# Two decode layers on one core: first keys as whole heads, w_down in four parts, last feed-forward in column halves, output turned on VectorE

## The chip, the cores and the metric

The kernel runs on one core of a Trainium2 chip. The metric is the device time of one execution in microseconds, lower is better; five executions of the kernel were timed. The profile shows one execution of its own: its span runs from the first to the last instruction, and its time is a little longer than its span.

## The reference, cut to what matters

Batch 4, one new token each, width D = 512, 32 query heads and 8 key/value heads of 128, 4096 cached positions, feed-forward width F = 1792. The same attention and feed-forward (same weights, same caches) are applied twice in a row. Softmax has scale 128 ** -0.5, gelu is the tanh approximation, and the layer norm has no gain or offset.

```python
def reference(A_x, A_k_cache, A_v_cache, A_wq, A_wo, B_x, B_w_gate, B_w_up, B_w_down):
    def _A_ref(x, k_cache, v_cache, wq, wo):
        q = (x @ wq).reshape(B, Sq, Hq, Dh).transpose(0, 2, 1, 3)
        k = jnp.repeat(k_cache, rep, axis=1)
        v = jnp.repeat(v_cache, rep, axis=1)
        scores = jnp.einsum("bhqd,bhkd->bhqk", q, k) * (Dh ** -0.5)
        o = jnp.einsum("bhqk,bhkd->bhqd", _softmax(scores), v)
        return o.transpose(0, 2, 1, 3).reshape(B, Sq, Hq * Dh) @ wo
    def _B_ref(x, w_gate, w_up, w_down):
        return (_gelu(x @ w_gate) * (x @ w_up)) @ w_down
    x = A_x
    for _ in range(2):
        x = x + _A_ref(_layernorm(x), A_k_cache, A_v_cache, A_wq, A_wo)
        x = x + _B_ref(_layernorm(x), B_w_gate, B_w_up, B_w_down)
    return x
```

## The kernel before

**Stages.** Each batch element has its own keys and values, some 8.4 MB of each, and they are too many to keep. So the kernel interleaves the two layers. `attend(None, 0)` (L498) does the first layer's attention of element 0. Then the loop at L679 does, for each element b, `dense(b, 1, ...)` (L660: rest of the output projection, layer norm, feed-forward), the query of the second layer, and `attend(b, b + 1, ...)`: the second layer's scores of element b against keys that still lie in SBUF, and the first layer's attention of element b + 1. `attend_last` (L618) ends the second layer's attention of element 3, and `dense(0, B, ...)` (L705) does the second feed-forward for all four elements at once. Values are read twice, once for each layer, and keys once.

**Order of work.** Nothing is scheduled by a tool: `tc.manual_schedule()` (L81) leaves the order of each engine as the program writes it. All loads go out on SP's queue (`dq`, L83) in program order, and a load waits there until its buffer is free. Work of one element's second layer is mixed by hand into the other's first layer: `fill(n)` in `dense` does n V tiles of the second layer, `vals.step(n)` n V tiles of the first.

**Keys.** A key head is two tiles of 128 partitions x 16 positions x 128 (512 KB, 4 KB a partition), `KT[head][t]` (L90). `Keys.load` (L361 on, issue at L365) issues them and `Keys.turn` (L367) transposes a tile in place in 32-bit blocks on VectorE (L372). Both run through `Keys.tile` (L356): per group of four heads, first t = 0 of the four, then t = 1. `scores(sc, g, t)` (L377) multiplies the four heads of a group for one t. For element 0, `attend` issues wq of group 0, the eight key tiles of group 0, wq of group 1, the eight of group 1, and then V tiles (L540 to L544).

**Values.** V tiles have seven buffers; `load_v` (L454) issues loads for as long as there is a free one, and `Values.step` (L467) frees one after its 16 matmuls (L481). In `attend_last` the key buffers serve for V tiles too (L625).

**Weights.** `load_rest` (L124) loads wo in four parts, w_gate and w_up whole, and w_down in three parts of 7, 4 and 3 row blocks of 128 rows. It is called in element 0's attention, after its last V tile is issued (L601).

**Feed-forward.** `ffn_in` (L300) has two forms. For one element, the activation is the stationary operand and the results are rows spread over the partitions, which `turn_rows` (L214) transposes on VectorE (L215). For four elements, the weights are the stationary operand and the result comes in columns (L307). `gelu` (L321) takes the columns through VectorE and ScalarE's tanh (L330), `gate_up` (L335) multiplies in the up half, and `down` (L343) runs 14 x 4 matmuls (L347). The layer norm's factor is made by `ln_rstd` (L183) in ten small VectorE instructions (L185 to L200), called in `dense` as an argument of `gelu`, which transposes the gate rows on entry:

```python
        sq, h = gelu(nb, rg, ln_rstd(nb, mv))
        H_bf = gate_up(nb, sq, h, ru)
```

**End.** The state `XX` holds the activations with the width on partitions. At the end `xoT` copies it to bf16 (L708), four transposes on TensorE put the batch on partitions (L711), VectorE copies them out of PSUM (L713), and SP stores 4 rows of 1 KB (L714).

## Time and profile before

| What | us |
| --- | --- |
| median of five runs | 316.14 |
| lowest and highest of them | 313.99, 318.96 |
| profiled execution, its own time | 318.96 |
| its span | 317.2 |
| TensorE matmuls busy | 213.7 (67%) |
| VectorE busy | 171.2 (54%) |
| ScalarE busy | 28.9 (9%) |
| 118 V tiles, median from issue to landing | 8.8 |
| 64 key tiles, median from issue to landing | 10.2 |

In the profile's lines, PE is a matmul and PEld its weight load, DVE is VectorE, ACT ScalarE, and SPq the issue of a DMA on SP's queue. A line of the timeline gives start and duration in us, engine, source line, operation, what it writes and reads with their shapes, a count, and in brackets how long the engine was idle before it and what ended that. A line of groups gives count, then busy us in total and mean ns of one. PEclk is the clock that TensorE was granted as a share of full, and the mean over the span was 0.692. Parts of a line's name can stand for several buffers, since buffer numbers are left out. An engine's busy share is a mean over stages with different limits, so stages are read one by one.

### The profile page before, as it was taken

How to read it: one execution, taken by the hardware profiler on the slowest of the kernel's cores; microseconds unless marked ns; L12 is line 12 of the kernel's file. 1: busy time of each engine (PE TensorE's matmuls, PEld its weight loads, DVE VectorE, ACT ScalarE, POOL GpSimd, SP SyncE). 2: the span in 40 equal slices, each digit the busy share in tenths (PEclk: the TensorE clock that was granted, in tenths of full speed). 3: DMA queues.
4: the chain of work that ended last, by engine and by line, in shares of the span. 5: the costliest groups of instructions: out<-in, count | busy, mean ns of one | idle time of the engine just before them, and what ended most of it. 6: DMA issues, size and time to landing. Idle time of an engine off the chain costs nothing.

```text
span 317.2 us, 8714 instructions
## 1 busy us (share of the span) xinstructions
PE 213.7 (67%) x3844; PEld 122.5 (39%) x3844; DVE 171.2 (54%) x481; ACT 28.9 (9%) x70; POOL 0.7 (0%) x6
## 2 busy tenths in 40 slices
PE   1460585343576669889946389699563797998875
PEld 0010344121324135656431246464421365645654
DVE  5575751023438896355378943354598552545133
ACT  0002010000002021200100212000202040003100
POOL 0000000000000000000000000000000000000000
PEclk9999999999998555555675555555855555559555
DMA  6999999999949999999999999999999999999910
GB/s 251 397 411 396 406 411 401 351 379 383 389 133 387 400 410 403 352 396 397 321 402 408 409 406 349 374 355 333 413 408 409 410 398 341 399 393 365 395 44 3
DMA packets 35527, 114.09 MB, mean 360 GB/s; under 512 B 3225, under 2 KB 9121, under 8 KB 35489
## 3 DMA queue, kind: packets, MB, share of 16 engines
q1 hardware_dynamic: 35488, 113.53, 94.2%
q8 instruction: 30, 0.49, 0.6%
q14 instruction: 9, 0.07, 0.0%
HBM read 113.51 MB, written 0.00 MB: 358 GB/s over the span
## 4 chain that ended last, share of the span: by engine, by line
DMA 46%; PE 25%; DVE 15%; SPq 8%; issue 3%; ACT 2%; DVEq 0%; ACTq 0%
DMA kt<-in_A_k_cache_dram 22%; DMA v<-in_A_v_cache_dram 21%; PE sc L383 6%; PE ot L481 6%; DVE kt L372 5%; DMA wd_sb<-in_B_w_down_dram 3%; SPq L127 3%; SPq L133 3%; PE rows L280 3%; PE rows L314 3%; PE y L347 2%; PE rows L225 2%; PE x L429 1%; DVE pp L410 1%; DVE rows L215 1%
## 5 line engine op out<-in xcount | busy, mean ns | idle before, releaser
L481 PEld LDWEIGHTS <-v 128*128 128x128 bf16 x1920 | 59.8, 105 | 51.2 <-DMA v<-in_A_v_cache_dram 26.1
L372 DVE STREAM_TRANSPOSE kt<-kt 128x1024 f32<-128x1024 f32 x64 | 74.9, 1216 | 7.2 <-DMA kt<-in_A_k_cache_dram 7.1
L481 PE MATMUL ot<-pe,v 128*128 128x4 bf16 x1920 | 63.7, 167 | 18.8 <-DMA v<-in_A_v_cache_dram 17.8
L383 PE MATMUL sc<-kt,qb 128*32 128x512 bf16 x512 | 63.9, 553 | 15.4 <-DVE kt L372 11.6
L215 DVE STREAM_TRANSPOSE rows<-rows 128x512 f32<-128x512 f32 (+1 forms) x23 | 16.3, 708 | 39.7 <-PE rows L225 19.9
L383 PEld LDWEIGHTS <-qb 128*32 128x32 bf16 x512 | 17.4, 117 | 46.3 <-issue 33.9
L402 ACT ACTIVATE pp<-sc,nm 128x512 bf16<-128x512 f32 x16 | 11.0, 688 | 155.6 <-DVE junk L398 155.5
L489 DVE TENSOR_TENSOR OT_bf<-ot,rden 128x8 bf16<-128x8 f32 (+1 forms) x40 | 6.5, 163 | 34.2 <-PE ot L481 33.7
L429 PE MATMUL x<-pp,ident_bf 128*32 128x128 bf16 x256 | 9.1, 282 | 23.3 <-DVE pp L410 23.2
L280 PE MATMUL rows<-wo_sb,OT_bf 128*1 128x512 bf16 (+1 forms) x136 | 17.2, 611 | 7.3 <-DMA wo_sb<-in_A_wo_dram 6.3
L225 PE MATMUL rows<-wq_sb,xn_bf 128*1 128x512 bf16 (+1 forms) x160 | 18.9, 622 | 4.8 <-DMA wq_sb<-in_A_wq_dram 4.5
L429 PEld LDWEIGHTS <-ident_bf 128*32 128x32 bf16 x256 | 6.7, 121 | 29.4 <-issue 27.8
L389 DVE TENSOR_REDUCE m<-sc 128x1 f32<-128x512 f32 x16 | 10.8, 676 | 12.1 <-PE sc L383 12.1
L410 DVE STREAM_TRANSPOSE pp<-pp 128x512 bf16<-128x512 bf16 x16 | 11.2, 702 | 4.7 <-ACT pp L402 4.3
L432 ACT CAST pe<-x 128x512 bf16<-128x512 f32 x16 | 9.4, 585 | 20.0 <-PE x L429 20.0
L246 PE MATMUL qe<-qm,t_bf 128*128 128x64 bf16 x16 | 3.5, 218 | 11.4 <-DVE qm L236 6.3
L347 PE MATMUL y<-H_bf,wd_sb 128*128 128x1 bf16 (+1 forms) x280 | 8.5, 166 | 2.7 <-DVE H_bf L340 1.5
L249 DVE TENSOR_TENSOR qb<-qe,amask 128x256 bf16<-128x256 f32 x16 | 6.8, 425 | 5.9 <-PE qe L246 5.9
L347 PEld LDWEIGHTS <-wd_sb 128*128 128x128 bf16 x280 | 8.1, 104 | 4.0 <-DMA wd_sb<-in_B_w_down_dram 3.0
L225 PEld LDWEIGHTS <-xn_bf 128*1 128x1 bf16 (+1 forms) x160 | 4.4, 110 | 13.1 <-issue 12.0
L415 PE MATMUL den<-zx,mean_f 128*128 128x16 f32 x32 | 8.9, 357 | 0.0
L420 DVE RECIPROCAL rden<-den 128x16 f32<-128x16 f32 x16 | 4.0, 251 | 8.5 <-PE den L415 8.0
(78 smaller groups left out, 125.0 us busy)
## 6 DMA issues: line engine op xcount, KB each, us to landing
v<-in_A_v_cache_dram SPq DMA_DIRECT2D x118, 512.0 KB, 8.8
kt<-in_A_k_cache_dram SPq DMA_DIRECT2D x64, 512.0 KB, 10.2
wq_sb<-in_A_wq_dram SPq DMA_DIRECT2D x2, 2048.0 KB, 7.8
wo_sb<-in_A_wo_dram SPq DMA_DIRECT2D x4, 1024.0 KB, 11.8
kt<-in_A_v_cache_dram SPq DMA_DIRECT2D x8, 512.0 KB, 10.4
wg_sb<-in_B_w_gate_dram SPq DMA_DIRECT2D x1, 1792.0 KB, 13.5
wu_sb<-in_B_w_up_dram SPq DMA_DIRECT2D x1, 1792.0 KB
wd_sb<-in_B_w_down_dram SPq DMA_DIRECT2D x1, 896.0 KB, 16.0
```

The lines of the kernel that those rows point to most:

```text
L127: dq.dma_start(out=wo_sb[:, i * n:(i + 1) * n], in_=wo_dram[:, i * n:(i + 1) * n])
L215: nc.vector.transpose(out=rows[:, :n], in_=rows[:, :n])
L225: nc.tensor.matmul(rows[j * QS:j * QS + nb, :], lhsT=xn_bf[:, k, bs], rhs=w, start=(k == 0), stop=(k == KD - 1))
L280: nc.tensor.matmul(rows[r0:r0 + lhsT.shape[-1], :], lhsT=lhsT, rhs=wo_sb[:, i, :], start=(start and n < QD), stop=(stop and n >= hp - QD))
L347: nc.tensor.matmul(y[:, k], lhsT=wd_sb[:, c, k * P:(k + 1) * P], rhs=H_bf[:, c, :], start=(c == 0 and k == 0), stop=(c == KF - 1), skip_gr ...
L372: nc.vector.transpose(out=words, in_=words)
L383: nc.tensor.matmul(sc[s * QS:(s + 1) * QS], lhsT=qb[:, w0:w0 + 2 * W], rhs=kt[:, :, be // 2, :, be % 2], start=(t == 0 and be == 0), stop= ...
L389: nc.vector.tensor_reduce(out=m[:], in_=sc.rearrange("p c j -> p (c j)"), axis=AX.X, op=ALU.max)
L402: nc.scalar.activation(out=pp[:], in_=sc[:], func=ACT.Exp, bias=nm[:, 0:1], scale=scale, accum_out=ls[:])
L410: nc.vector.transpose(out=flat, in_=flat)
L429: nc.tensor.matmul(x[a * QS:(a + 1) * QS, s], lhsT=ident_bf[:, s * QS:(s + 1) * QS], rhs=pT[:, a], start=True, stop=True, skip_group_check ...
L481: nc.tensor.matmul(self.ot[:, s % 2], lhsT=v[:, i, :], rhs=pe[:, s, c, :], start=(c == 0), stop=(c == C - 1), skip_group_check=True)
```

## The change

1. **Element 0's keys as whole heads.** The two tiles of a head become halves of one buffer `KH[head]`. Element 0's heads are loaded by `load_whole`, one load of 1 MB (8 KB a partition) each. `Keys.tile` runs head by head for element 0, and `attend` spreads the turns anew: seven before the first scores, one before the second, and so on. For later elements the loads are those of before.
2. **w_down in four parts** of 7, 3, 3 and 1 row blocks.
3. **Feed-forward functions.** `ffn_in` keeps only its row form. `gelu` now takes the turned gate columns as an argument ahead of the layer norm's factor, and writes into tiles that are made outside.
4. **The last feed-forward** is written out: gate in two halves of 7 column blocks, then gelu in two halves, then for each half the up matmuls and `gate_up`. `down` is as before.
5. **The last V tile** is loaded in two parts of 8 positions each.
6. **The output** is added straight into a bf16 tile `xo` with 16 used columns, turned by four 32 x 32 transposes on VectorE, and stored as 16 rows of 256 bytes.

```diff
@@ -87,7 +87,8 @@
     wg_sb = wts.tile([P, KD, F], BF16, name="wg_sb")
     wu_sb = wts.tile([P, KD, F], BF16, name="wu_sb")
     wd_sb = wts.tile([P, KF, D], BF16, name="wd_sb")
-    KT = [[wts.tile([P, CH, Dh], BF16, name=f"kt{i}_{t}") for t in range(NT)] for i in range(Hkv)]
+    KH = [wts.tile([P, C, Dh], BF16, name=f"kt{i}") for i in range(Hkv)]
+    KT = [[KH[i][:, t * CH:(t + 1) * CH] for t in range(NT)] for i in range(Hkv)]
     wq_dram = A_wq.rearrange("(k p) n -> p k n", p=P)
     wo_dram = A_wo.rearrange("(i p) n -> p i n", p=P)
 
@@ -97,6 +98,8 @@
     OT2_bf = state.tile([P, Hq, B], BF16, name="OT2_bf")
     q1_bf = state.tile([P, NG, NK, B], BF16, name="q1_bf")
     xn_bf = state.tile([P, KD, B], BF16, name="xn_bf")
+    xo = state.tile([P, QS], BF16, name="xo")
+    xr = state.tile([QS, P], BF16, name="xr")
     qb = state.tile([P, W + NK * 2 * W], BF16, name="qb")
 
     ROWS = [ps_row.tile([P, 512], FP32, name=f"rows{i}") for i in range(2)]
@@ -114,8 +117,11 @@
     def groups(b):
         return [b % NG, (b + 1) % NG]
 
+    def cache_rows(cache, b, kvh, c0, n):
+        return cache[b, kvh].rearrange("(p c) d -> p c d", p=P)[:, c0:c0 + n]
+
     def cache_tile(cache, b, kvh, t):
-        return cache[b, kvh].rearrange("(p c) d -> p c d", p=P)[:, t * CH:(t + 1) * CH]
+        return cache_rows(cache, b, kvh, t * CH, CH)
 
     def load_wq(g):
         n = HG * Dh
@@ -128,7 +134,7 @@
         dq.dma_start(out=wg_sb[:], in_=B_w_gate.rearrange("(k p) n -> p k n", p=P))
         dq.dma_start(out=wu_sb[:], in_=B_w_up.rearrange("(k p) n -> p k n", p=P))
         wd_dram = B_w_down.rearrange("(k p) n -> p k n", p=P)
-        cuts = [0, KF // 2, KF - 3, KF]
+        cuts = [0, KF // 2, KF - 4, KF - 1, KF]
         for lo, hi in zip(cuts, cuts[1:]):
             dq.dma_start(out=wd_sb[:, lo:hi], in_=wd_dram[:, lo:hi])
 
@@ -138,6 +144,7 @@
         for r in ROWS:
             nc.vector.memset(r[:], 0.0)
         nc.vector.memset(qb[:], 0.0)
+        nc.vector.memset(xo[:], 0.0)
         nc.vector.tensor_reduce(out=amask[:], in_=ident_bf[:].rearrange("p (a i) -> p a i", a=QD),
                                 axis=AX.X, op=ALU.max)
         nc.vector.tensor_reduce(out=s32_f[:], in_=ident_bf[:].rearrange("p (a i) -> p i a", a=QD),
@@ -297,48 +304,39 @@
             nc.vector.tensor_tensor(out=XX[:, 0, bs], in0=XX[:, 0, bs],
                                     in1=y.rearrange("p k b -> p b k"), op=ALU.add)
 
-    def ffn_in(b0, nb, w_sb, cols):
+    def ffn_in(b0, nb, w_sb):
         bs = slice(b0, b0 + nb)
         rows = new_rows()
-        if cols:
-            h = rows[:, :KF * nb].rearrange("p (c j) -> p c j", j=nb)
-            for c in range(KF):
-                for k in range(KD):
-                    nc.tensor.matmul(h[:, c], lhsT=w_sb[:, k, c * P:(c + 1) * P],
-                                     rhs=xn_bf[:, k, bs], start=(c == 0 and k == 0),
-                                     stop=(k == KD - 1), skip_group_check=True)
-            return h, cols
         for k in range(KD):
             w = w_sb[:, k].rearrange("p (n a i) -> p a n i", a=QD, i=QS)
             for j in range(QD):
                 nc.tensor.matmul(rows[j * QS:j * QS + nb, :KF * QS], lhsT=xn_bf[:, k, bs],
                                  rhs=w[:, j], start=(k == 0), stop=(k == KD - 1))
-        return rows, cols
-
-    def ffn_cols(h, nb):
-        return h[0] if h[1] else turn_rows(h[0], KF * QS)[:, :, :nb]
-
-    def gelu(nb, rows, rstd):
-        hg = ffn_cols(rows, nb)
-        h = small.tile([P, KF, nb], FP32, name="h", tag="h")
-        nc.vector.tensor_tensor(out=h[:], in0=hg, in1=spread_rstd(rstd, KF, nb), op=ALU.mult)
-        sq = small.tile([P, KF, nb], FP32, name="sq", tag="sq")
+        return rows
+
+    def ffn_cols(rows, nb):
+        return turn_rows(rows, KF * QS)[:, :, :nb]
+
+    def gelu(nb, hg, rstd, sq, h):
+        n = h.shape[1]
+        nc.vector.tensor_tensor(out=h[:], in0=hg, in1=spread_rstd(rstd, n, nb), op=ALU.mult)
         nc.vector.scalar_tensor_tensor(out=sq[:], in0=h[:], scalar=0.044715, in1=h[:],
                                        op0=ALU.mult, op1=ALU.mult)
         nc.vector.scalar_tensor_tensor(out=sq[:], in0=sq[:], scalar=1.0, in1=h[:],
                                        op0=ALU.add, op1=ALU.mult)
         nc.scalar.activation(out=sq[:], in_=sq[:], func=ACT.Tanh, scale=GELU_C)
         nc.vector.scalar_tensor_tensor(out=h[:], in0=h[:], scalar=0.5,
-                                       in1=spread_rstd(rstd, KF, nb), op0=ALU.mult, op1=ALU.mult)
-        return sq, h
-
-    def gate_up(nb, sq, h, rows):
-        hu = ffn_cols(rows, nb)
+                                       in1=spread_rstd(rstd, n, nb), op0=ALU.mult, op1=ALU.mult)
+
+    def ffn_tiles(nb):
+        sq = small.tile([P, KF, nb], FP32, name="sq", tag="sq")
+        h = small.tile([P, KF, nb], FP32, name="h", tag="h")
+        return sq, h, small.tile([P, KF, nb], BF16, name="H_bf", tag="H_bf")
+
+    def gate_up(hu, sq, h, H_bf):
         nc.vector.scalar_tensor_tensor(out=sq[:], in0=sq[:], scalar=1.0, in1=h[:],
                                        op0=ALU.add, op1=ALU.mult)
-        H_bf = small.tile([P, KF, nb], BF16, name="H_bf", tag="H_bf")
         nc.vector.tensor_tensor(out=H_bf[:], in0=hu, in1=sq[:], op=ALU.mult)
-        return H_bf
 
     def down(nb, H_bf):
         y = ps_sm.tile([P, KD, nb], FP32, name="y", tag="sm")
@@ -355,14 +353,20 @@
 
         def tile(self, n):
             o, u = divmod(n, TG)
-            t, s = divmod(u, GH)
+            s, t = divmod(u, NT) if self.b == 0 else divmod(u, GH)[::-1]
             return groups(self.b)[o] * GH + s, t
+
+        def load_whole(self, count):
+            for _ in range(count):
+                kvh = self.tile(self.nl)[0]
+                self.nl += NT
+                dq.dma_start(out=KH[kvh][:], in_=cache_rows(A_k_cache, self.b, kvh, 0, C))
 
         def load(self, count):
             for _ in range(count):
                 kvh, t = self.tile(self.nl)
                 self.nl += 1
-                dq.dma_start(out=KT[kvh][t][:], in_=cache_tile(A_k_cache, self.b, kvh, t))
+                dq.dma_start(out=KT[kvh][t], in_=cache_tile(A_k_cache, self.b, kvh, t))
 
         def turn(self, count=1):
             for _ in range(count):
@@ -458,7 +462,10 @@
                 return
             seen["load"] += 1
             v = held[b, g, s, t] = free.pop(0)
-            dq.dma_start(out=v[:], in_=cache_tile(A_v_cache, b, g * GH + s, t))
+            n = CH // 2 if seen["load"] == len(loads) else CH
+            for c in range(0, CH, n):
+                dq.dma_start(out=v[:, c:c + n],
+                             in_=cache_rows(A_v_cache, b, g * GH + s, t * CH + c, n))
 
     class Values:
         def __init__(self, b, last, prob, dst):
@@ -538,9 +545,9 @@
                 load_v()
         else:
             load_wq(0)
-            keys.load(TG)
+            keys.load_whole(GH)
             load_wq(1)
-            keys.load(TG)
+            keys.load_whole(GH)
             load_v()
             make_identity(nc, ident_bf[:])
             build_consts()
@@ -552,14 +559,15 @@
             rstd1 = ln_rstd(B, ln_center(0, B))
             q_first(q_rows(0, B, 0), 0, rstd1)
             build_q1(0, 0)
-            turn(4)
+            turn(TG - 1)
         sc1 = new_scores(0)
         scores(sc1, ga, 0)
-        turn(4)
+        turn(1 if first else GH)
         if two:
             vals2.step(max(early[b2] - vals2.n - 1, 0))
         scores(sc1, ga, 1)
-        turn()
+        if two:
+            turn()
         p0 = soft(sc1)
         turn()
         if two:
@@ -569,13 +577,15 @@
         turn()
         prob1[ga] = (pe, soft_recip(den))
         if first:
+            turn()
             q_first(q_rows(0, B, 1), 1, rstd1)
         build_q1(b1, gb)
-        turn()
+        turn(5 if first else 1)
         vals.step(2)
         sc1 = new_scores(0)
         scores(sc1, gb, 0)
-        turn(4)
+        if two:
+            turn(4)
         vals.step(3)
         scores(sc1, gb, 1)
         rows = new_rows()
@@ -665,11 +675,12 @@
         ln_square(b0, nb)
         mv = ln_center(b0, nb)
         fill(1)
-        rg = ffn_in(b0, nb, wg_sb, nb > 1)
+        rg = ffn_in(b0, nb, wg_sb)
         fill(1)
-        ru = ffn_in(b0, nb, wu_sb, nb > 1)
-        sq, h = gelu(nb, rg, ln_rstd(nb, mv))
-        H_bf = gate_up(nb, sq, h, ru)
+        ru = ffn_in(b0, nb, wu_sb)
+        sq, h, H_bf = ffn_tiles(nb)
+        gelu(nb, ffn_cols(rg, nb), ln_rstd(nb, mv), sq, h)
+        gate_up(ffn_cols(ru, nb), sq, h, H_bf)
         fill(2)
         add_y(b0, nb, down(nb, H_bf))
 
@@ -702,16 +713,35 @@
         else:
             proj = attend_last(b, next_q, fill)
 
-    dense(0, B, proj, lambda n: None)
-
-    xoT = state.tile([P, KD, B], BF16, name="xoT")
-    nc.vector.tensor_copy(out=xoT[:], in_=XX[:, 0].rearrange("p b k -> p k b"))
-    xo_ps = ps_sm.tile([P, D], BF16, name="xo_ps", tag="sm")
-    for k in range(KD):
-        nc.tensor.transpose(xo_ps[:B, k * P:(k + 1) * P], xoT[:, k, :], ident_bf[:, :])
-    xo = tmpp.tile([P, D], BF16, name="xo", tag="pp")
-    nc.vector.tensor_copy(out=xo[:B, :], in_=xo_ps[:B, :])
-    nc.sync.dma_start(out=out.flatten_outer_dims(), in_=xo[:B, :])
+    def ffn_part(w_sb, h, c0, c1):
+        for c in range(c0, c1):
+            for k in range(KD):
+                nc.tensor.matmul(h[:, c], lhsT=w_sb[:, k, c * P:(c + 1) * P], rhs=xn_bf[:, k, :],
+                                 start=(c == 0 and k == 0), stop=(k == KD - 1),
+                                 skip_group_check=True)
+
+    out_proj_end(*proj)
+    add_y(0, B, proj[0])
+    ln_square(0, B)
+    mv = ln_center(0, B)
+    hg, hu = [new_rows()[:, :KF * B].rearrange("p (c j) -> p c j", j=B) for _ in range(2)]
+    parts = [(0, KF // 2), (KF // 2, KF)]
+    for c0, c1 in parts:
+        ffn_part(wg_sb, hg, c0, c1)
+    rstd = ln_rstd(B, mv)
+    sq, h, H_bf = ffn_tiles(B)
+    for c0, c1 in parts:
+        gelu(B, hg[:, c0:c1], rstd, sq[:, c0:c1], h[:, c0:c1])
+    for c0, c1 in parts:
+        ffn_part(wu_sb, hu, c0, c1)
+        gate_up(hu[:, c0:c1], sq[:, c0:c1], h[:, c0:c1], H_bf[:, c0:c1])
+    y = down(B, H_bf)
+    nc.vector.tensor_tensor(out=xo[:, :B * KD].rearrange("p (b k) -> p b k", k=KD),
+                            in0=XX[:, 0], in1=y.rearrange("p k b -> p b k"), op=ALU.add)
+    for a in range(QD):
+        nc.vector.transpose(out=xr[:, a * QS:(a + 1) * QS], in_=xo[a * QS:(a + 1) * QS, :])
+    nc.sync.dma_start(out=out.flatten_outer_dims().rearrange("b (k c) -> (b k) c", k=KD),
+                      in_=xr[:B * KD, :])
 
 
 # ---- launch: one core; inputs and outputs as the reference has them ----
```

## The prediction

> **What bounds the kernel now.** I read the page's DMA rows first, then stretches of the trace by rate, then the chain that ended last, and last the instruction timeline where the diff touches it. The page's transfer rows (share of the 16 DMA engines in tenths, and GB/s, in 40 slices of 7.93 us):
>
> ```profile
> DMA  6999999999949999999999999999999999999910
> GB/s 251 397 411 396 406 411 401 351 379 383 389 133 387 400 410 403 352 396 397 321 402 408 409 406 349 374 355 333 413 408 409 410 398 341 399 393 365 395 44 3
> ```
>
> The transfers are busy nearly everywhere: 113.5 MB at some 400 GB/s. Two stretches are not theirs: slice 11 (87 to 95 us), and the end from 302 us. The table of stretches gives rates by row size (last column GB/s, the one before it DMA share; the first number is the stretch, in us):
>
> ```profile
> 4.00:10.00 6.00, 1.51 (x14) 0.83 (x18) 1.91 (x12) 0.00 (x0) 0.00 (x0) 1.00 1.03 418
> 12.00:24.00 12.00, 6.92 (x33) 1.79 (x34) 9.68 (x10) 0.00 (x0) 0.00 (x0) 1.00 1.03 415
> 58.00:66.00 8.00, 2.24 (x20) 0.55 (x23) 0.00 (x0) 0.00 (x0) 0.00 (x0) 1.00 1.10 348
> 88.00:92.00 4.00, 3.33 (x33) 1.18 (x37) 0.52 (x2) 0.00 (x0) 0.00 (x0) 1.00 0.12 40
> 302.00:317.00 15.00, 9.32 (x254) 7.73 (x250) 5.60 (x27) 0.25 (x1) 0.00 (x0) 0.50 0.04 15
> ```
>
> wq comes at 418, the first keys in 512 KB tiles (4 KB a partition) at 415, wo (1 KB rows) at 348. At 88 to 92 us there is a hole: the chain of waits runs from the landing of w_down's last part (83.08 us, 12 matmuls, 0.49 us) through compute until scores free the key tiles (first new key load 90.83 us). The chain's last wait on a transfer is a V tile that landed at 269.1 us; from there to the end it is compute alone. So before 83 us transfers set the time, 83 to 91 us is compute, the middle is transfers with compute close behind, and the last 48 us are compute.
>
> **The change, part by part.** The sum is made in the profiled execution (span 317.2 us, its own time 318.96, so 1.8 us lie around the span) and the difference is carried to the median, 316.14.
>
> *First keys as whole heads.* 16 key loads become 8 of 1 MB. SP issues half as many; nothing behind them starves, since 512 KB tiles already took 13.6 us (median) from issue to landing, so many are in flight. VectorE turns head by head, so the first scores wait for the seventh turn (12.89 + 7 x 1.14 = 20.9 us instead of 14.18), yet the eighth still ends at 22.0, and the softmax no longer waits for a second-group key (26.35 us). None of this reaches the end: the second group's last scores (43.14 us) stand behind a V tile on PE that landed at 42.6 us, and key turns (done 42.5 us) become some 4 us earlier, not the tile. Without that cover a head would cost one more 1.2 us turn. What is left is the rate. From the rows: 1 KB costs one engine 1024 x 16 / 348 = 47 ns, 4 KB 158 ns, so 10 ns fixed; 8 KB then 306 ns, 429 GB/s, and 8.39 MB take 19.6 us instead of 20.2: -0.65. The other end is 0, if 8 KB goes as two of 4 KB. I take -0.3. [...]
>
> *w_down in four parts.* One DMA more on SP, and the last part is one row block instead of three: after its landing 4 matmuls instead of 12, 0.49 x 8/12 = 0.33 us off the head of the hole's chain. A smaller last transfer may land a little later (bounds -0.35 to +0.2): -0.3. It shifts everything behind the hole.
>
> *A step moved, which the description does not name.* `gelu(nb, ffn_cols(rg, nb), ln_rstd(nb, mv), ...)` builds the turn of the gate rows before the ten instructions of `ln_rstd`; VectorE's instruction order shows it for all four per-element feed-forwards. Before, the fourth one reads:
>
> ```profile
> 271.03 0.16 DVE L200 SCALAR_TENSOR_TENSOR rstd<-r,rstd 128x1 f32<-128x1 f32 x1
> 271.42 0.67 DVE L215 STREAM_TRANSPOSE rows<-rows 128x448 f32<-128x448 f32 x1 [0.23 <-PE rows L314]
> 272.12 0.17 DVE L324 TENSOR_TENSOR h<-rows,rstd 128x14 f32<-128x14 f32 x1
> ...
> 273.53 0.67 DVE L215 STREAM_TRANSPOSE rows<-rows 128x448 f32<-128x448 f32 x1 [0.62 <-PE rows L314]
> 274.11 0.15 DVE L337 SCALAR_TENSOR_TENSOR sq<-sq,h 128x14 f32<-128x14 f32 x1
> 274.30 0.17 DVE L340 TENSOR_TENSOR H_bf<-rows,sq 128x14 bf16<-128x14 f32 x1
> ```
>
> rstd is done at 271.2, under the gate matmuls, and the turn starts when they end. Now ten instructions at 0.195 us a step (1.95 us) come behind the turn: h at 272.10 + 1.95 = 274.05, four steps of 0.21, up turn at 274.88 instead of 273.53: +1.35. Queued behind it on VectorE is H_bf, and PE's 56 down matmuls wait for that. For the third element likewise 206.51 + 0.70 + 1.95 + 0.83 = 209.99 against 208.62: +1.37; for the second 143.09 against 142.08: +1.01. For the first, 75.04 + 3.48 = 78.5 against 79.58, when w_up's matmuls end after their late landing (77.87): hidden, 1.0 us to spare.
> What carries? The fourth: everything, +1.35, since no transfer ends a wait behind it (the last V tile is used at 305.06, and transfers stop about 302.3). Second and third: a V or key load goes out later, but loads issued at 148 to 149 us took 6.5 to 7.3 us to land, at 212 to 216 us 8.5 to 9.1: five to seven tiles of 1.28 us in flight, of which one is lost. VectorE idles for the next keys anyway (1.3 and 1.5 us). Bounds 0 and 2.4; I take +0.5, near the hidden end, because rates there already sag (326 GB/s at 150 to 160 us).
>
> *The end.* VectorE, PE and SP, in order:
>
> ```profile
> 310.03 0.22 DVE L324 TENSOR_TENSOR h<-rows,rstd 128x56 f32<-128x56 f32 x1
> 311.42 0.22 DVE L340 TENSOR_TENSOR H_bf<-rows,sq 128x56 bf16<-128x56 f32 x1
> 311.69 1.64 PE L347 MATMUL y<-H_bf,wd_sb 128*128 128x4 bf16 x56 [0.41 <-DVE H_bf L340]
> 313.36 0.17 DVE L297 TENSOR_TENSOR XX<-XX,y 128x16 f32<-128x16 f32 x1 [1.72 <-PE y L347]
> 313.57 0.17 DVE L708 CAST xoT<-XX 128x16 bf16<-128x16 f32 x1
> 314.42 0.41 DVE L713 COPY xo<-xo_ps 4x512 bf16<-4x512 bf16 x1 [0.68 <-PE xo_ps L711]
> 314.86 0.29 SPq L714 DMA_DIRECT2D out_dram<-xo  x1
> ```
>
> h waits for rstd, which ends at 309.93, not for the gate matmuls (over at 309.6); so two halves gain nothing and double VectorE's instructions from 6 to 12. A step is 0.25 us at 56 columns and 0.21 at 14: 0.22 at 28. The first half of H_bf is tenth in order: 310.03 + 9 x 0.22 + 0.19 = 312.20, PE starts at 312.25 instead of 311.69: +0.56. The second half is ready at 312.64, before PE needs it (313.07).
> Output: XX to the store's issue took 1.50 us. Now one add (0.21), four 32x32 turns, 0.03. The nearest row is the softmax's small turn:
>
> ```profile
> L392 DVE STREAM_TRANSPOSE mt<-m 128x32 f32<-128x32 f32 x16 | 3.4, 212 | 0.6
> ```
>
> Four at 0.22: 1.12 us, -0.38. [...] 16 rows of 256 B instead of 4 of 1 KB: no row, 0, at most 0.3 either way. Together +0.2.
>
> *At nothing.* The last V tile in two loads: PE reaches it at 305.06, 2.8 us after transfers stop; with that cover gone it gains half a tile (0.64 us). The memset of `xo` (0.06 us) lies before the wait for wq at 9.01.
>
> Sum: -0.3 - 0.3 + 0.5 + 1.35 + 0.2 = +1.45, so 317.6 us, 0.5% above the median.
>
> **Rivals.** *All three moved chains show*: -0.3 - 0.3 + 1.01 + 1.37 + 1.35 + 0.2 = +3.3, 319.5 us. For: the sagging rates at 150 to 160 and 210 to 220 us. Against: five to seven tiles in flight. *None shows*, with V tiles ending last at the fourth too: -0.4, 315.7 us. For: two of PE's weight loads in the last part name a V tile. Against: the chain has none after 269 us. *Faster: whole heads uncover a cost per transfer* at 2 to 36 us. It decides above 1.45 / 8 = 0.18 us for each of the eight transfers saved; at 0.6 us it makes -3.3, 312.8 us. Against: no stretch there lacks transfers in flight, and the best rate seen is 418. *The clock*: PE's granted clock falls to 0.5 from 102 us on; if the moved work alters its few stretches at 1.0, the ends shift by 1 to 2 us either way.
>
> **How the numbers follow.** Forecast 0.5, all three show 0.2, none shows 0.15, faster by transfers 0.06, clock 0.09. The five runs of before spread from 313.99 to 318.96, so a per cent (3.2 us) is about what can be told from no change. Slower by over 1%: half of "all three" and some of the rest, 0.23; faster: 0.06; within: 0.71. The unknown terms alone (-0.65 to 0, -0.35 to +0.2, 0 to 2.4, -0.6 to +0.5 around the end) and the medians' scatter give 314.8 to 320.4.
>
> **What would show it.** In the changed profile: the first 36 us at 415 to 430 GB/s; 4 matmuls after w_down's last landing and the first new key load near 90.5; ln_rstd behind the gate turn and down starting 1.0 to 1.4 us later against the gate matmuls; first H_bf half about 2.2 us after rstd; four turns in 0.9 us. Wrong if the fourth feed-forward's delay is taken up by a later V wait, or if key rates rise well past 430.

## The result, and the profile after

The changed kernel takes 318.2 us (median of 43 runs, 312.85 to 322.27) beside 316.97 us for the kernel before on the same chip (80 runs, 313.52 to 321.3). The ratio is 1.0002, with a 95% interval of 0.9981 to 1.0023: +0.1 us, between -0.6 and +0.7. The ratio is taken over the runs within 1.5% of each kernel's own fastest, so disturbed runs are left out and one fast run moves it; the medians over all runs stand 0.4% apart. The profiled execution took 319.35 us with a span of 317.6 (before: 318.96 and 317.2).

The change as a whole thus moved the time by less than can be told. Its parts did not: the traces show gains of some 1.7 us and losses of some 3 us in it. First the page's transfer rows of the changed kernel (busy tenths and GB/s, slices of 7.94 us), and a row of its table of transfers:

```profile
DMA  7999999999869999999999999999999999999900
GB/s 255 425 415 422 412 417 408 350 393 372 333 190 402 409 417 411 324 415 328 305 408 410 417 410 341 400 357 336 360 411 413 417 401 357 417 340 381 369 16 3
...
kt<-in_A_k_cache_dram SPq DMA_DIRECT2D x8, 1024.0 KB, 15.8
```

The second to the fifth slice (8 to 40 us) were 397, 411, 396 and 406; now they are 425, 415, 422 and 412. The hole at 87 to 95 us went from 133 to 190 GB/s. The table of stretches (stretch, its length, busy time of PE, its weight loads, VectorE, ScalarE and GpSimd, granted TensorE clock, DMA share, GB/s) puts it more closely:

```profile
9.00:11.00 2.00, 1.88 (x16) 0.37 (x15) 0.07 (x1) 0.00 (x0) 0.00 (x0) 1.00 1.03 434
12.00:24.00 12.00, 5.05 (x33) 1.70 (x34) 9.68 (x10) 0.00 (x0) 0.00 (x0) 1.00 1.02 415
24.00:36.00 12.00, 3.68 (x40) 1.33 (x34) 9.47 (x16) 2.95 (x5) 0.00 (x0) 1.00 1.01 417
```

The same stretches of the kernel before, of which only 12 to 24 us was shown (415 in both kernels, so in the middle of the key loads nothing was gained):

```profile
9.00:11.00 2.00, 1.88 (x16) 0.38 (x15) 0.07 (x1) 0.00 (x0) 0.00 (x0) 1.00 0.99 338
...
24.00:36.00 12.00, 2.96 (x34) 1.33 (x34) 6.78 (x13) 2.96 (x5) 0.00 (x0) 1.00 1.02 399
```

At 9 to 11 us, where the loads pass from wq to keys, the rate fell to 338 GB/s at a DMA share of 0.99, so the transfer engines were busy and yet slow; that dip is gone. Added up, 13.78 MB have arrived by 36 us instead of 13.28, and PE's first matmul on a V tile starts at 36.37 us instead of 37.51. Later, the first new key load goes out at 88.82 instead of 90.83. The load edits are not all of these 2.0 us: with both of them alone on the kernel before it goes out at 89.62.

Another gain comes from none of the load edits. At 40 to 50 us, when V tiles arrive, the eight kernels built on the changed one (the one with 1 MB loads of 4 KB rows apart, which falls to 397 at 45 to 48 us and 291 at 48 to 51) run at 417 to 419 GB/s, also the one with half-head keys, and the five built on the kernel before at 407 to 409, also those with whole heads. 10 GB/s over 10 us are 0.1 MB, some 0.25 us. Its source was not found.

Those 2 us are gone by the store: it is issued at 315.19 us against 314.86. The first loss is the moved `ln_rstd`. The instruction timeline of the fourth feed-forward, changed kernel (start, duration, engine, line, operation; in brackets the idle time and what ended it):

```profile
269.53 0.67 DVE L222 STREAM_TRANSPOSE rows<-rows 128x448 f32<-128x448 f32 x1 [1.91 <-PE rows L313]
270.11 0.14 DVE L192 TENSOR_TENSOR msq<-mv 128x1 f32<-128x1 f32 x1
271.83 0.16 DVE L207 SCALAR_TENSOR_TENSOR rstd<-r,rstd 128x1 f32<-128x1 f32 x1
272.02 0.17 DVE L322 TENSOR_TENSOR h<-rows,rstd 128x14 f32<-128x14 f32 x1
272.74 0.66 DVE L222 STREAM_TRANSPOSE rows<-rows 128x448 f32<-128x448 f32 x1
273.49 0.17 DVE L339 TENSOR_TENSOR H_bf<-rows,sq 128x14 bf16<-128x14 f32 x1
273.72 1.65 PE L345 MATMUL y<-H_bf,wd_sb 128*128 128x1 bf16 x56 [1.18 <-DVE H_bf L339]
```

VectorE idled 1.91 us before the gate turn, the very time in which it used to make rstd; now rstd comes behind the turn, and down starts 4.19 us after the turn's start instead of 3.10 (271.42 us in the kernel before, and then):

```profile
274.52 1.65 PE L347 MATMUL y<-H_bf,wd_sb 128*128 128x1 bf16 x56
```

The second loss is at the end. The same view there:

```profile
309.25 0.89 PE L719 MATMUL rows<-xn_bf,wu_sb 128*128 128x4 bf16 x28
...
311.46 0.19 DVE L339 TENSOR_TENSOR H_bf<-rows,sq 128x28 bf16<-128x28 f32 x1
311.70 0.89 PE L719 MATMUL rows<-xn_bf,wu_sb 128*128 128x4 bf16 x28 [1.56 <-DVE H_bf L339]
312.44 1.63 PE L345 MATMUL y<-H_bf,wd_sb 128*128 128x4 bf16 x56
312.62 0.19 DVE L339 TENSOR_TENSOR H_bf<-rows,sq 128x28 bf16<-128x28 f32 x1 [0.88 <-PE rows L719]
314.11 0.17 DVE L739 TENSOR_TENSOR xo<-XX,y 128x16 bf16<-128x16 f32 x1 [1.31 <-PE y L345]
314.32 0.84 DVE L742 STREAM_TRANSPOSE xr<-xo 32x32 bf16<-32x32 bf16 x4
315.19 0.35 SPq L743 DMA_DIRECT2D out_dram<-xr  x1
```

The up matmuls come in two groups of 28. The second starts 1.56 us after the first ended, 0.05 us after VectorE finished the *first* H_bf half, with which it has no data in common except that both sit in one PSUM tile: VectorE reads columns 0 to 27 of `hu` while PE would write 28 to 55. Down stands behind it on PE. So the path is the first H_bf half, the second up group, then down, and the up group was not in the forecast's sum. The four output turns take 0.84 us, as forecast.

### The profile page after: what moved, and what is told of

Same layout as the page of the kernel before. It is cut to its first block, busy times and chain, and to the rows that moved or that the text cites. A ratio compares the mean times of both kernels' runs of the same rounds, so it can differ in the third digit from the quotient of the medians.

```text
span 317.6 us, 8714 instructions
## 1 busy us (share of the span) xinstructions
PE 211.2 (67%) x3840; PEld 122.2 (38%) x3840; DVE 172.5 (54%) x490; ACT 29.1 (9%) x71; POOL 0.7 (0%) x6
## 4 chain that ended last, share of the span: by engine, by line
DMA 48%; PE 24%; DVE 15%; SPq 8%; issue 3%; ACT 1%; DVEq 0%; ACTq 0%
DMA v<-in_A_v_cache_dram 23%; DMA kt<-in_A_k_cache_dram 22%; PE sc L387 7%; PE ot L488 6%; DMA wd_sb<-in_B_w_down_dram 3%; SPq L139 3%; PE rows L287 3%; SPq L133 3%; DVE kt L376 2%; PE y L345 2%; DVE rows L222 2%; PE rows L232 2%; PE rows L313 2%; PE x L433 1%; SPq L134 1%
## 5 line engine op out<-in xcount | busy, mean ns | idle before, releaser
L387 PE MATMUL sc<-kt,qb 128*32 128x512 bf16 x512 | 62.3, 549 | 18.5 <-DVE kt L376 14.5
L232 PE MATMUL rows<-wq_sb,xn_bf 128*1 128x512 bf16 (+1 forms) x160 | 18.9, 621 | 4.6 <-DMA wq_sb<-in_A_wq_dram 4.3
L327 ACT ACTIVATE sq<-sq 128x14 f32<-128x14 f32 (+1 forms) x6 | 1.3, 218 | 84.1 <-DVE sq L325 84.1
```

The lines of the kernel that those rows point to most:

```text
L232: nc.tensor.matmul(rows[j * QS:j * QS + nb, :], lhsT=xn_bf[:, k, bs], rhs=w, start=(k == 0), stop=(k == KD - 1))
L387: nc.tensor.matmul(sc[s * QS:(s + 1) * QS], lhsT=qb[:, w0:w0 + 2 * W], rhs=kt[:, :, be // 2, :, be % 2], start=(t == 0 and be == 0), stop= ...
```

## The experiments

All twelve kernels were timed beside the kernel before. The medians of the kernel before were 315.95 us for the first four experiments, 316.15 for the next four and 316.59 for the last four. Two traced distances carry most of the readings: from the add of an element's output projection to the add of its feed-forward, and, at the end, from the last output projection's add to the store's issue. The second is pure compute and repeats to 0.02 us between traces of like kernels. The diffs show the lines that matter; the changes that follow from them (turn order, helper functions) are left out.

### The loads

**Keys alone.** The kernel before with whole-head key loads and the order of turns that goes with them.

```diff
-            keys.load(TG)
+            keys.load_whole(GH)
```

> The kernel before with one part of the change, element 0's keys as whole heads with their turn order. Theory A (whole heads bring the early loads in sooner; the prediction's -0.3 us was too small): the last w_down matmul of element 0 ends near 82.0 us instead of 83.57, and the time falls by 1.2 to 1.8 us (ratio 0.995). Theory B (the sizes of the prediction hold and the 2 us that lie between the two profiled executions at 83 us are scatter): that matmul ends at 83.0 to 83.6, the time falls by 0.3 us or less (ratio 0.999).

Measured: 316.05 us, ratio 1.0011 (0.9986 to 1.0036). In its trace 13.69 MB have come by 36 us, the first V matmul is at 36.53 and the first new key load at 90.20 (before: 13.28 MB, 37.51, 90.83). The last w_down matmul ends at 82.93 us, between the two theories, and the time (+0.3 us, -0.4 to +1.1) fits B: the gain is in the trace and not in the total.

**Keys left as they were.** The changed kernel with half-head loads and the turns of before.

```diff
-            keys.load_whole(GH)
+            keys.load(TG)
```

> The kernel after with the loads and turn order of before for element 0's keys (half heads), all else changed. Theory A: the last w_down matmul moves back to 83.0 to 83.3 us and the time rises by 1.2 to 1.8 us against the changed kernel (ratio 1.005 to the kernel before). Theory B: it stays where the changed kernel has it within 0.3 us, ratio 1.001.

Measured: 319.85 us, ratio 1.0094 (1.0067 to 1.0122). 13.28 MB by 36 us, first V matmul 37.55, first new key load 90.15. The trace goes with A: the last w_down matmul ends at 82.89 us, where the changed kernel has 81.55. How far the time does is discussed under "The changed kernel once more".

Over all traces the first V matmul lies at 36.2 to 36.8 us in the nine kernels with whole heads and at 37.4 to 37.9 in the four with half heads (the next kernel, at 38.87, is apart). Whole heads are worth about 1.1 us there.

**Large loads with short rows.** The changed kernel with eight key loads of 1 MB, each the same half of two heads, so rows of 4 KB as before; turns in the order of before.

```diff
-                dq.dma_start(out=KH[kvh][:], in_=cache_rows(A_k_cache, self.b, kvh, 0, C))
+                src = A_k_cache[self.b, kvh:kvh + 2].rearrange("h (p c) d -> p h c d", p=P)
+                dq.dma_start(out=KP[kvh // 2][:, :, c0:c0 + CH], in_=src[:, :, c0:c0 + CH])
```

> The kernel after, but the eight 1 MB key loads of element 0 each take the same half of two heads (4 KB rows) instead of one whole head (8 KB rows), with the turn order of before. If the number of transfers and the bytes in flight make the gain, it stays as in the changed kernel: last w_down matmul near 81.6 us, ratio 1.000. If the length of the rows makes it, the gain is lost: 83.0 to 83.3 us, ratio 1.005. Theory B: no difference from the changed kernel beyond 0.3 us.

Measured: 321.65 us, ratio 1.0146 (1.0086 to 1.0206). Its table of stretches:

```profile
9.00:11.00 2.00, 1.66 (x16) 0.37 (x15) 0.00 (x0) 0.00 (x0) 0.00 (x0) 1.00 1.04 358
12.00:24.00 12.00, 4.46 (x19) 1.19 (x20) 8.64 (x10) 0.00 (x0) 0.00 (x0) 1.00 1.03 414
24.00:36.00 12.00, 3.98 (x40) 1.59 (x43) 7.17 (x12) 2.95 (x5) 0.00 (x0) 1.00 1.03 411
```

As many transfers as with whole heads, and as large, but the dip stays (358) and 13.40 MB have come by 36 us, a quarter of the way from 13.28 to 13.78. So for the dip it is the row of 8 KB, not the number or size of the transfers. Nor is it that loads enter the queue sooner: SP issues the second wq load at 10.25 us in the kernel before, at 3.64 with whole heads, and here, with the dip, at 3.94. At 24 to 36 us this kernel has 411, nearer to 417 than to 399, so there the size may have a part. The ratio fits neither theory: this kernel was slow later too (322 and 284 GB/s at 50 to 58 us), which isn't explained.

**w_down in three parts.** The changed kernel with the old cuts.

```diff
-        cuts = [0, KF // 2, KF - 4, KF - 1, KF]
+        cuts = [0, KF // 2, KF - 3, KF]
```

> The kernel after with w_down in three parts as before. Theory A and B alike, from the prediction: 12 matmuls instead of 4 after the last landing, the first new key load 0.3 us later, time up by 0.3 us (ratio 1.001). A rival: the small last part costs a landing of its own and nothing changes, or the time falls by 0.1 to 0.2 us.

Measured: 320.54 us, ratio 1.0105 (1.0074 to 1.0137), far above the 0.3 us that was expected. The trace does not explain it: the first new key load goes out at 89.57 us, 0.75 later than in the changed kernel's first trace and 0.38 later than in its second. **Both load changes on the kernel before**, nothing else:

```diff
-            keys.load(TG)
+            keys.load_whole(GH)
-        cuts = [0, KF // 2, KF - 3, KF]
+        cuts = [0, KF // 2, KF - 4, KF - 1, KF]
```

> The kernel before with only the two early load edits, whole heads and w_down in four parts. Theory A (whole heads save 1.1 us by their longer rows, w_down 0.3 us, and both reach the end): first new key load at 89.1 instead of 90.8 us, ratio 0.9956. Rival (the later stages take the gain back, since transfers set the time again): first new key load at 89.1 us all the same, ratio 0.999 to 1.001.

Measured: 316.92 us, ratio 0.9994 (0.9959 to 1.0029), which is the rival's: the gain does not show in the total. The first new key load goes out at 89.62 us, 1.2 earlier than before. How w_down lands is seen in PE's timeline, changed kernel:

```profile
78.91 1.39 PE L345 MATMUL y<-H_bf,wd_sb 128*128 128x1 bf16 x40 [1.13 <-DVE H_bf L339]
80.92 0.63 PE L345 MATMUL y<-H_bf,wd_sb 128*128 128x1 bf16 x16 [0.62 <-DMA wd_sb<-in_B_w_down_dram]
```

and, kernel before:

```profile
80.67 0.89 PE L347 MATMUL y<-H_bf,wd_sb 128*128 128x1 bf16 x28 [1.13 <-DVE H_bf L340]
81.96 0.58 PE L347 MATMUL y<-H_bf,wd_sb 128*128 128x1 bf16 x16 [0.41 <-DMA wd_sb<-in_B_w_down_dram]
83.08 0.48 PE L347 MATMUL y<-H_bf,wd_sb 128*128 128x1 bf16 x12 [0.54 <-DMA wd_sb<-in_B_w_down_dram]
```

16 matmuls follow the last wait, not 4: the third part (three blocks) landed so late that PE took it together with the fourth. Counted from the issue of w_down's first part, down ends after 18.9 to 19.1 us in the nine kernels with four parts and after 19.1 to 19.3 in the five with three (before: 64.38 to 83.56, 19.18). So four parts gain about 0.2 us, by their landing, not by fewer matmuls behind it: the last wait ends 18.40 us after that issue in the changed kernel and 18.70 before.

### The moved step

**rstd first.** The changed kernel, with the step put back ahead of the turn in all four per-element feed-forwards.

```diff
-        gelu(nb, ffn_cols(rg, nb), ln_rstd(nb, mv), sq, h)
+        rstd = ln_rstd(nb, mv)
+        gelu(nb, ffn_cols(rg, nb), rstd, sq, h)
```

> The kernel after with the ten instructions of the layer norm's factor ahead of the gate turn again, in all four per-element feed-forwards. Theory A (the moved step costs what the fourth feed-forward shows, and the second and third are mostly taken up by loads in flight): the down matmuls of the fourth start 1.1 us sooner behind the gate turn, the time falls by 1.1 to 1.6 us (ratio 0.996). Rival (all three show): it falls by 3.0 us (ratio 0.990). Rival (none shows): 1.000.

Measured: 315.11 us, ratio 0.994 (0.9905 to 0.9975), 2.0 us under the changed kernel's ratio: between theory A and the rival in which all three show. The fourth feed-forward takes 8.08 us from add to add, where the changed kernel has 9.19.

**The fourth, doubled.** The kernel before; for the last element alone the turn comes first and then `ln_rstd` twice (the first result is overwritten, the output is the same).

```diff
+        if nb == 1 and b0 == 3:
+            hg = ffn_cols(rg, nb)
+            rstd = ln_rstd(nb, mv)
+            rstd = ln_rstd(nb, mv)
```

> The kernel before with the same doubled factor behind the gate turn in the fourth per-element feed-forward only. Theory A (everything behind it is compute, so all of it shows): the time rises by 2.9 to 3.2 us (ratio 1.0095). Rival (V tiles end last there too, and take it up): below 1 us (ratio 1.003).

Measured: 319.38 us, ratio 1.0121 (1.0089 to 1.0153), that is +3.8 us (2.8 to 4.8). Its timeline:

```profile
270.44 0.67 DVE L215 STREAM_TRANSPOSE rows<-rows 128x448 f32<-128x448 f32 x1 [2.14 <-PE rows L314]
...
275.46 0.66 DVE L215 STREAM_TRANSPOSE rows<-rows 128x448 f32<-128x448 f32 x1
...
276.45 1.65 PE L346 MATMUL y<-H_bf,wd_sb 128*128 128x1 bf16 x56 [3.00 <-DVE H_bf L339]
```

Down comes 6.01 us after the turn's start (before: 3.10), +2.9. From the last element's output projection to the store is 49.98 us (before: 314.86 - 267.76 = 47.10), +2.9 again: nothing behind the fourth takes it up.

**The second and third, doubled.** The same for those two elements.

```diff
+        if nb == 1 and b0 in (1, 2):
+            hg = ffn_cols(rg, nb)
+            rstd = ln_rstd(nb, mv)
+            rstd = ln_rstd(nb, mv)
```

> The kernel before with the layer norm's factor behind the gate turn and computed twice, in the second and third per-element feed-forwards only. Each of the two is then 2.9 us longer. If loads in flight take a delay up there (theory A: the prediction gave 0.5 of 2.4 us for the single one), the time rises by 0.5 to 1.5 us (ratio 1.002 to 1.005). If such delays show (rival), it rises by 5 to 6 us (ratio 1.017).

Measured: 320.89 us (6 runs), ratio 1.0113 (1.0061 to 1.0166), +3.6 us (1.9 to 5.3). The two feed-forwards take 11.30 and 11.45 us (before 8.70 and 8.44), together +5.6. The output projection of the last element, the first step after them that waits for V tiles, is only +1.7 later than before (269.47 against 267.76), or +2.65 against the kernel with only the fourth doubled (266.82). So neither all nor nothing: a third to two thirds show.

### The end

**Both up halves ahead of the chain.** The changed kernel with all up matmuls written before the first `gate_up`; the halves on VectorE stay.

```diff
     for c0, c1 in parts:
         ffn_part(wu_sb, hu, c0, c1)
+    for c0, c1 in parts:
         gate_up(hu[:, c0:c1], sq[:, c0:c1], h[:, c0:c1], H_bf[:, c0:c1])
```

> The kernel after with both halves of the last up matmuls issued ahead of both halves of the gated product. Theory A (the second up half waits for VectorE to have read the first, 1.56 us of PE idle, and so down starts 0.6 us late): PE doesn't idle between the up halves, down starts 2.3 us after the factor instead of 2.9, time down by 0.6 us (ratio 0.998). Rival (the twelve VectorE instructions alone set it): no change.

Measured: 318.85 us, ratio 1.0047 (1.0014 to 1.0079). Its timeline:

```profile
309.70 1.63 PE L719 MATMUL rows<-xn_bf,wu_sb 128*128 128x4 bf16 x56
309.82 0.16 DVE L207 SCALAR_TENSOR_TENSOR rstd<-r,rstd 128x4 f32<-128x4 f32 x1
...
312.15 1.63 PE L345 MATMUL y<-H_bf,wd_sb 128*128 128x4 bf16 x56 [0.81 <-DVE H_bf L339]
...
314.89 0.35 SPq L744 DMA_DIRECT2D out_dram<-xr  x1
```

The 56 up matmuls run in one group under VectorE's chain and the wait is gone. From the last output projection's add (306.56) to the store it is 8.33 us, where the changed kernel has 9.08: the wait costs 0.75. The timing does not show it (1.0047 beside the changed kernel's 1.0002); the claim rests on this distance.

**The last feed-forward whole.** The changed kernel with one part instead of two.

```diff
-    parts = [(0, KF // 2), (KF // 2, KF)]
+    parts = [(0, KF)]
```

> The kernel after with the last feed-forward whole, six VectorE instructions instead of twelve. Theory A: down starts 1.76 us after the factor instead of 2.9, time down by 1.15 us (ratio 0.9965). The prediction's size: 0.56 us (ratio 0.998). Rival (halves help on a busier PE): it rises.

Measured: 319.02 us, ratio 1.0021 (0.9985 to 1.0057). The same distance is 7.94 us, 1.14 less than in the changed kernel, as theory A had it. The timing's interval is too wide to show that.

**Both mends.** rstd first and the last feed-forward whole; loads and output turn stay as changed.

```diff
-        gelu(nb, ffn_cols(rg, nb), ln_rstd(nb, mv), sq, h)
+        rstd = ln_rstd(nb, mv)
+        gelu(nb, ffn_cols(rg, nb), rstd, sq, h)
-    parts = [(0, KF // 2), (KF // 2, KF)]
+    parts = [(0, KF)]
```

> The kernel after with the layer norm's factor first and the last feed-forward whole: what is left of the change is whole heads, w_down in four parts, the V tile in two loads and the output on VectorE. Theory A: -1.6 (keys) - 0.3 (w_down) - 0.4 (output) = 2.3 us under the kernel before, ratio 0.993. Theory B (keys only 0.3): 1.0 us under it, ratio 0.997.

Measured: 314.31 us, ratio 0.9937 (0.991 to 0.9965), -2.0 us (-2.8 to -1.1): as theory A had it, and faster than both kernels. Its end:

```profile
302.47 0.17 DVE L304 TENSOR_TENSOR XX<-XX,y 128x16 f32<-128x16 f32 x1 [0.66 <-PE y L293]
...
307.65 1.64 PE L345 MATMUL y<-H_bf,wd_sb 128*128 128x4 bf16 x56 [0.41 <-DVE H_bf L339]
309.32 0.17 DVE L740 TENSOR_TENSOR xo<-XX,y 128x16 bf16<-128x16 f32 x1 [1.72 <-PE y L345]
309.53 0.84 DVE L743 STREAM_TRANSPOSE xr<-xo 32x32 bf16<-32x32 bf16 x4
310.40 0.35 SPq L744 DMA_DIRECT2D out_dram<-xr  x1
```

310.40 - 302.47 = 7.93 us, where the kernel before has 314.86 - 306.51 = 8.35.

**The changed kernel once more**, beside the doubled steps.

> The changed kernel itself once more, beside the three others on one chip, so that their ratios can be set against it. Theory A: 1.000 to 1.002, with the store's issue 9.1 us behind the last output projection's sum.

Measured: 319.51 us (313.38 at the lowest), ratio 1.0004 (0.9961 to 1.0047). By the medians over all runs it stands 2.9 us above the kernel before here, and stood 1.2 above in the first timing. This also says how to read the kernels that differ from it only in their loads: their medians stand 3.9 us (half-head keys) and 4.6 us (w_down in three parts) above that of before, so only some 1.0 and 1.7 us above the changed kernel as timed here (2.7 and 3.4 above it as timed first). Its own place moves by more than these differences, so they size nothing.

## Why the prediction was right, and where its terms were not

The forecast was 317.6 us, +1.45, most likely within 1% of before, and within 1% it is. Its mechanism, small gains against the moved step, is the one seen. The size is in part luck: +1.45 lies outside the ratio's interval (-0.6 to +0.7) and between what the medians give (+1.2, and +2.9 when timed again), and two terms missed in opposite directions, the keys by 0.8 us in trace and the end by 0.6. Of its signs, rstd behind the gate turn, down 1.0 to 1.4 us later (+1.09), the first H_bf half 2.2 us after rstd (309.53 to 311.65) and four turns in 0.9 us (0.84) came; the first new key load at 90.5 (88.82) and 4 matmuls after w_down's last landing (16) did not. The loads' rate reached 434 GB/s at 9 to 11 us and was 415 to 417 in the two stretches after it. Its terms:

| term | forecast us | measured us | from |
|---|---|---|---|
| keys as whole heads | -0.3 (-0.65 to 0) | -1.1 | first V matmul |
| w_down in four parts | -0.3 | -0.2 | issue to the end of down |
| ln_rstd late, 2nd and 3rd | +0.5 of 2.4 | +0.6 to +1.2 of 1.8 | doubled step |
| ln_rstd late, 4th | +1.35 | +1.0 | traces, doubled step |
| last feed-forward in halves | +0.56 | +1.14 | last add to store |
| output turn | -0.38 | -0.41 | last add to store |
| V tile in two loads, memset | 0 | no wait seen | timeline of the end |
| sum | +1.45 | +1.0 to +1.6 | |

**Keys: mis-sized.** The step "10 ns fixed" per row, fitted from the 1 KB and 4 KB rates, gave 429 GB/s at best, halved for doubt. The doubt, that 8 KB might go as two of 4 KB, was needless: 8 KB rows do go as single packets. The pages of the changed kernel and of before count:

```profile
DMA packets 34558, 114.09 MB, mean 359 GB/s; under 512 B 3156, under 2 KB 9048, under 8 KB 33496
DMA packets 35527, 114.09 MB, mean 360 GB/s; under 512 B 3225, under 2 KB 9121, under 8 KB 35489
```

So 1,024 packets more are of 8 KB or larger, which are 8 loads of 128 rows. But the saving per row is not what came: at 12 to 24 us the rate is 415 with rows of either length. The gain lies where the forecast did not look, first of all in the dip at 9 to 11 us, which was in the trace of before. That dip is 0.19 MB, 0.5 us, about half of the gain; the other half is 417 for 399 GB/s at 24 to 36 us. 1 MB loads with 4 KB rows brought a quarter of the gain by 36 us (13.40 MB), so most of it is not a cost saved per load. The faster rival (decided above 0.18 us per saved transfer) got 1.1 / 8 = 0.14, and mostly from another cause.

**w_down: size about right, reason wrong.** The forecast's 4 matmuls behind the last landing are 16.

**The moved step.** The fourth shows in full, as said; the mean of seven traces with late rstd is 9.3 us for this feed-forward and of six with early rstd 8.3. In the changed kernel's own trace, turn to down is +1.09 instead of +1.35: the ten instructions start 0.58 us after the turn's start, not 0.70, and the up turn 0.09 us after the instruction before it, not 0.21. For the second and third, 1.8 us in the changed trace are a third of the 5.6 us of the doubled step, so +3.6 us becomes +1.2 (0.6 to 1.8), and the later output projection +0.6 to +0.9. The forecast's +0.5 leaned a little too far towards "hidden"; how much lies within the scatter of the stretches in which transfers set the time. The first is hidden, as forecast: VectorE still idles 1.26 us before the up turn (77.83 us).

**The end: the step that failed** is "+0.56" for the halves, with "The second half is ready at 312.64, before PE needs it". The VectorE part was fair: with both up halves ahead, the halves cost 8.33 - 7.94 = 0.39 us. But between the halves PE writes the PSUM tile that VectorE reads, and waits. The waits view of the changed kernel names it in one row (what waits, for what, us in total, times, longest):

```profile
PE rows L719 <- DVE H_bf L339: 1.6, 1, 1.6
```

Most of these 1.6 us are time in which PE had nothing better to do; 0.75 are lost. The kernel's text already holds it: both up halves are written into the one tile `hu`, and the first half's `gate_up`, which reads it, stands between them. The forecast had counted VectorE's instructions and not looked at PE's. That the shared tile is the reason is argued from this text and the wait's name; halves in two tiles were not tried. Shown is that the order makes the wait, since with both up halves first it is gone.

**The output turn** is right at the value of the row chosen: 212 ns a turn in the kernel before, four in 0.84 us (0.21 each) in seven traces with these turns. The lower end of "-0.6 to +0.5 around the end" reckons with turns of less than half of that; no run shows such a term.

**The clock**, a rival at 0.09, moved and the time did not follow. In eight of the traces TensorE's granted clock stays at 1.00 until about 100 us; in the other six, all of kernels with whole heads, it falls to 0.50 at about 28 us. The rows of the kernel before and of the changed kernel's second trace (40 slices, tenths):

```profile
PEclk9999999999998555555675555555855555559555
PEclk9997555555567555565855555657655555559555
```

The early fall (mean clock of the execution near 0.59 instead of 0.69) came in 123 of 217 executions of the nine kernels with whole heads and in none of 235 of the others, the kernel before among them. So the loads bring it on, how is not shown. Of the changed kernel, 19 executions with it and 25 without have the same median, 318.2 us; in the other kernels now the one kind has the lower median, now the other.

**What the terms make of the other kernels.** Each kernel's sum, with +0.9 for the second and third, beside its ratio turned into us (the doubled kernels gave terms, and the one with 4 KB rows is left out as unexplained):

| kernel | sum us | timed us (95%) |
|---|---|---|
| changed | +1.3 | +0.1 (-0.6 to +0.7); again +0.1 (-1.2 to +1.5) |
| keys alone | -1.1 | +0.3 (-0.4 to +1.1) |
| both loads alone | -1.3 | -0.2 (-1.3 to +0.9) |
| changed, half-head keys | +2.4 | +3.0 (2.1 to 3.9) |
| changed, w_down in three | +1.5 | +3.3 (2.3 to 4.3) |
| changed, rstd first | -0.6 | -1.9 (-3.0 to -0.8) |
| changed, up first | +0.6 | +1.5 (0.4 to 2.5) |
| changed, feed-forward whole | +0.2 | +0.7 (-0.5 to +1.8) |
| changed, both mends | -1.7 | -2.0 (-2.8 to -1.1) |

Signs and order hold broadly, single kernels miss by up to 1.8 us one way and 1.3 the other. **What stays open** is whether the loads' 1.3 us, plain in the traces up to 90 us, reach the end. The two kernels with nothing but the loads show no gain; both mends, at -2.0, does. Without that term the changed kernel would be at +2.6, rstd first at +0.7 and both mends at -0.4, all further from their timings, but the other five would be nearer to theirs, so the table doesn't decide. Nor can single traces: from the first new key load to the last element's output projection, the four traces that are alike up to there (changed, twice; up first; feed-forward whole) take 172.9 to 177.9 us, and these 5 us are most of what sets the four executions apart (313.38 to 320.28 us). A run of all three load variants side by side would be needed. Half-size loads with 8 KB rows (a head split by partitions), which would part row from size from the other side, weren't tried either.

## What to carry to other kernels

When a call is rewritten, read the order of the instructions that each engine gets, since an argument's place in a call can move ten instructions from under a matmul to behind it, and its cost was full (2.9 us of 2.9, the doubled fourth) where only compute followed. Splitting a short chain into halves gained nothing here (it cost 0.39 us on VectorE), because the first half's input was not the thing waited for, and it cost 0.75 us more because the second half's writer waited for the first half's reader; look at the waits of the engine that fills the tile, not only at the instructions of the one that reads it. A total near zero says little about its parts: here, taking out two parts of the change gave a kernel 0.6% faster than before (0.991 to 0.9965).

## What the runs showed of the hardware that was not expected

- Rows of 8 KB ran at 418 to 431 GB/s at 9 to 12 us in nine kernels, where 4 KB rows, lying 8 KB apart, gave 302 to 362 in four kernels with 512 KB loads and 371 with 1 MB loads. At 12 to 24 us both ran at 414 to 418.
- In two traces of the changed kernel TensorE's granted clock fell from 1.00 to 0.50 at about 28 us in the one and only at about 100 us in the other, and over its executions the time didn't follow (median 318.2 us with either); only kernels with whole-head loads showed the early fall, in 123 of 217 executions.
- Four turns of a 32x32 bf16 block took 0.84 us; halving a VectorE step from 56 columns to 28 took it from about 0.25 to 0.22 us only.
